# Moving the first batch's result stores from GpSimd's queue to SyncE's in a Fourier mixing and SwiGLU kernel

## The chip, the cores and the metric

The kernel runs on one core of one Trainium2 chip. The core has five engines that run side by side, each with its own in-order stream of instructions: TensorE (matmuls; "PE" in the profile), VectorE (DVE), ScalarE (ACT), GpSimd (POOL) and SyncE (SP, which only issues transfers). "SPq", "ACTq" and "POOLq" are what these engines' sequencers do: waits, and the issue of transfers. The metric is the device time of one execution in microseconds (us); lower is better. All data is float32.

## The reference

The first half filters every channel of every batch along the sequence in the frequency domain; the second half is a SwiGLU block over all tokens.

```python
x: (8, 3008, 256)   filt_r, filt_i: (1505, 256)
X = rfft(x, axis=1)
Y = X * (filt_r + 1j * filt_i)
y = irfft(Y, n=3008, axis=1)             # (8, 3008, 256)

t = y.reshape(24064, 256)
g = t @ w_gate                            # (256, 1536)
v = t @ w_val                             # (256, 1536)
out = (g * sigmoid(g) * v) @ w_out        # (24064, 256), float32
```

## The kernel before, in words

**Work and order.** The eight batches are taken one after the other (index `b`). A batch's sequence of 3008 is handled as 47 x 64, and the SwiGLU half is done on four chunks of tokens (`k` = 0..3) in three groups of hidden features (`g` = 0..2): twelve steps per batch. In batch 0 the order of the first nine steps is by group: chunks 0, 1, 2 of group 0, then of group 1, then of group 2 (steps 6, 7 and 8); chunk 3 follows in steps 9, 10 and 11. In all other batches a chunk's three groups follow each other.

**The written-out schedule.** Within a step the order is a list of tokens, `SCHEDULE`, walked in the last loop. A capital letter is usually a group of matmuls (`P`, `Q`, `A`, `B`, `E` hidden products, L1034; `W` output products, L1131), a small letter the work on another engine that goes with it. A prime means the work of an earlier step. The lines that matter below:

- `D` (L329, on GpSimd) subtracts two tiles that ScalarE made; VectorE's `s` and `x` (L1056) need `D`, and the hidden products `A` (tile `wa`) need those.
- `S` (L326 and L329, on GpSimd) combines hidden tiles `h` for the output products.
- `o` (L326, VectorE) adds output products to the result tile `o`, and `z` (L1102, VectorE) transposes it in 32 x 32 blocks.
- `t` tokens run a piece of the spectral work of the *next* batch. In batch 0, steps 6 to 10, these are `stage2a` (matmuls into `pb`, L870; then VectorE L879, L883, L886 and a GpSimd addition, all on parts of the tile `lent`) and `stage2b` (matmuls into `pc`, L903; ScalarE's copy L911; ScalarE's transfer `d<-lent`, L917). `stage2a` of unit u first calls `load_two` for unit u+1: through `load` (L596) SyncE issues one piece of a table (`later_tbl`), four of `filt_r`, two of `filt_i` and one of the intermediate `d`, all into `lent`. The matmuls of `stage2b` for unit u-2 stand just before those of `stage2a` for unit u. Each of the two uses the same single PSUM bank in turn.
- `i0` to `i11` are the stores of batch 0's finished results. Each is issued two steps after its group, at steps 8, 9, 10 and 13 (step 13 is the second step of batch 1): twelve stores of 30 or 32 rows x 16 x 32 values (60 or 64 KB), each made of runs of 32 values (128 bytes). In batches 1 to 7 the stores belong to other tokens (`x`) and go to SyncE's queue.
- In batch 1's first three steps ScalarE also negates parts of the filter (`negated_filter`): SyncE loads them (L318), ScalarE multiplies them by -1 (L321), SyncE stores them (L323).

**Queues and semaphores.** SyncE issues nearly all loads: weights (`wt_t<-w_all`, L477), saved sums (`y_t<-yt`, L1266), saved outputs (`o<-o`, L996), and those of `load_two`. An engine issues its transfers in the order in which the program records them, and one that waits holds back all behind it. The recording layer gives the transfers of SyncE and ScalarE *together* eight completion semaphores in turn (they are named DMAHW0 to DMAHW7 in the listing of the built program); a transfer that is given a semaphore first waits until the transfer that had it before has landed, which is usually the one eight places earlier in the common order. GpSimd's transfers have eight of their own (DMASW0 to DMASW7).

The choice of the queue, before:

```python
queue = nc.sync if b else nc.gpsimd
if last:
    queue = (nc.sync, nc.scalar, nc.gpsimd)[(2 * p + n) % 3]
```

Of the kernel before, what the change touches and what calls it, by code (L numbers as in the profile page):

```python
# [203 lines left out]
def kernel(  # L204
# [10 lines left out]
    nc = tc.nc  # L215
# [109 lines left out]
    def add(eng, dst, a, b):  # L325
        return eng.tensor_tensor(out=dst, in0=a, in1=b, op=ALU.add)  # L326
# [663 lines left out]
    def takes_turns(b, k):  # L990
        return b == 0 and k < NT

    def new_outs(b, k, g):
        outs[b, k] = opool.tile([128, 4 * NH, RP], FP32, name=f"o_{b}_{k}_{g}", tag="o", bufs=2)
        if g:
            pin(nc.sync.dma_start(out=outs[b, k], in_=o_dram[k]))  # L996
        else:
            pin(nc.gpsimd.memset(outs[b, k][:, :, NR:], 0.0))

    class Group:  # L1000
# [94 lines left out]
        def project(self, op, last=False):  # L1095

            b, k, q = self.b, self.k, self.g
            kind, p = op[0], int(op[1:].split(".")[0])
            if kind == "z":
                if q == NG - 1:  # L1100
                    t = self.part(p)
                    pin(nc.vector.transpose(out=t, in_=t))  # L1102
                return
            if kind in "xXi":
                t, first, count = outs[b, k], 2 * NH * (kind == "X"), 2 * NH if last else 4 * NH
                if kind == "x" and q < NG - 1 and takes_turns(b, k) and p == 5:
                    pin(nc.sync.dma_start(out=o_dram[k], in_=t))
                if q == NG - 1 and (b or kind == "i"):
                    some = (p,) if kind == "i" else (2 * p, 2 * p + 1)
                    for n, (u, cq) in enumerate(divmod(m, 4) for m in some):  # L1110
                        rows = min(32, NR - 32 * u)
                        at = (b * S + 32 * 32 * u + 2 * NH * k) * C + 128 * first + 32 * cq
                        queue = nc.sync if b else nc.gpsimd
                        if last:
                            queue = (nc.sync, nc.scalar, nc.gpsimd)[(2 * p + n) % 3]
                        pin(queue.dma_start(  # L1116
                            out=bass.AP(tensor=out.tensor, offset=out.offset + at,
                                        ap=[[32 * C, rows], [128, count], [1, 32]]),
                            in_=t[32 * cq:32 * cq + rows, first:first + count, ts(u, 32)]))
                return  # L1120
            if kind == "q":
                at, kind, p = "A", "o", 4
            else:
                at = {1: "A", 6: "A", 7: "A", 4: "F" if last else "A", 2: "F", 5: "G",
                      3: "G"}[p]
            if kind == "W":
                start = p in (1, 2, 5) or last and p == 4
                if start:
                    self.bank(at, 3)
                for i in range(JB):  # L1130
                    pin(nc.tensor.matmul(  # L1131
                        out=self.tiles[at], lhsT=wo_t[:, JB * q + i, WO[p], :],
                        rhs=self.hs[i][:, HID[p]], start=start and i == 0,
                        stop=True, skip_group_check=True))
                return
            if q == 0 and p == 1:
                new_outs(b, k, q)
            i, cb = {1: (0, 0), 2: (0, 0), 6: (0, 1), 3: (0, 1), 4: (1, 0), 7: (1, 1),
                     5: (1, 1)}[p]
            dst = self.part(2 * i + cb)[:, :, 0:NR].rearrange("p n (t r) -> p t n r", t=2)  # L1140
            src = self.tiles[at].rearrange("p (t n r) -> p t n r", t=2, n=NH)
            if q == 0 and at == "A":
                pin(nc.scalar.copy(out=dst, in_=src))
            else:
                pin(add(nc.vector, dst, dst, src))
# [316 lines left out]
```

## Time and profile before

The time is 2839.53 us, the median of three runs (2835.15 to 2841.27); the profiled execution has a span of 2837.5 us.

| engine | busy us | share of the span |
|---|---|---|
| PE (matmul) | 2789.6 | 98% |
| PEld (weight load, beside PE) | 2315.4 | 82% |
| DVE | 2035.0 | 72% |
| ACT | 1567.1 | 55% |
| POOL | 1525.2 | 54% |

The stretch in which batch 0's stores are issued is small: GpSimd issues them in four bursts, from 323.9, 359.7, 394.7 and 483.3 us. Steps 8, 9, 10 and 13 begin on TensorE at about 322, 357, 393 and 482 us. A step takes about 29 us where TensorE has no gaps (454.54 to 483.75 on the chain of waits, from one `wqa` to the next).

How to read the views: a timeline row is start, duration, engine, line, operation, output <- input and count, with the idle time just before it and what ended that idle time in brackets. A row of the waits is who waited for whom: total us, times, longest. A row of the chain of waits is start, duration and what ran. A row of the windows is the stretch, its length, then each engine's busy us and number of instructions, the granted TensorE clock (1.00 is full speed), the busy share of the transfer engines and GB/s.

### The profile page before, as it was taken

How to read it: one execution, taken by the hardware profiler on the slowest of the kernel's cores; microseconds unless marked ns; L12 is line 12 of the kernel's file. 1: busy time of each engine (PE TensorE's matmuls, PEld its weight loads, DVE VectorE, ACT ScalarE, POOL GpSimd, SP SyncE). 2: the span in 40 equal slices, each digit the busy share in tenths (PEclk: the TensorE clock that was granted, in tenths of full speed). 3: DMA queues.
4: the chain of work that ended last, by engine and by line, in shares of the span. 5: the costliest groups of instructions: out<-in, count | busy, mean ns of one | idle time of the engine just before them, and what ended most of it. 6: DMA issues, size and time to landing. Idle time of an engine off the chain costs nothing.

```text
span 2837.5 us, 48561 instructions
## 1 busy us (share of the span) xinstructions
PE 2789.6 (98%) x15432; PEld 2315.4 (82%) x15432; DVE 2035.0 (72%) x4603; ACT 1567.1 (55%) x4202; POOL 1525.2 (54%) x1671
## 2 busy tenths in 40 slices
PE   8999999999999999999999999999999999999998
PEld 6777878788888888888888888878888888888887
DVE  6898766767667776677766677667776767766666
ACT  6775445555555555555555555555555555555554
POOL 4886566454545554455544555444554454545543
PEclk9999999999999999999999999999999999999999
DMA  8687867877666775667666676667765777645443
GB/s 231 218 272 251 269 203 228 275 226 233 188 183 204 248 218 178 199 213 232 216 185 197 214 238 204 185 191 234 228 205 177 214 221 226 195 146 153 151 137 82
DMA packets 363372, 586.58 MB, mean 207 GB/s; under 512 B 198388, under 2 KB 246260, under 8 KB 363024
## 3 DMA queue, kind: packets, MB, share of 16 engines
q1 hardware_dynamic: 337922, 534.73, 60.6%
q10 hardware_dynamic: 23406, 45.43, 5.9%
q0 software_dynamic: 1792, 3.34, 0.5%
q8 instruction: 125, 2.05, 0.3%
q14 instruction: 127, 1.04, 0.1%
HBM read 467.87 MB, written 101.34 MB: 201 GB/s over the span
## 4 chain that ended last, share of the span: by engine, by line
PE 85%; DVE 4%; POOL 3%; issue 2%; DMA 1%; ACT 1%; SPq 0%; ACTq 0%; DVEq 0%; POOLq 0%
PE wa L1034 22%; PE wk L1034 16%; PE wA L1131 15%; PE we L1034 12%; PE wG L1131 8%; PE wF L1131 4%; PE pd L937 3%; PE wqa L690 2%; PE wqc L749 1%; PE wqb L761 1%; POOL out_dram L1116 1%; DVE y L333 1%; DVE lent L818 1%; POOL h L329 1%; DVE o L326 0%
## 5 line engine op out<-in xcount | busy, mean ns | idle before, releaser
L1034 PE MATMUL wa<-y_t,wt_t 128*128 128x188 f32 x4464 | 880.3, 323 | 6.3 <-DVE wa L1056 2.0
L1034 PEld LDWEIGHTS wa<-y_t,wt_t 128*128 128x128 f32 x4464 | 746.8, 190 | 84.9 <-ACT wa L1060 11.0
L1034 PEld LDWEIGHTS wk<-y,wt_t 128*128 128x128 f32 x2976 | 494.6, 190 | 106.7 <-issue 33.4
L1034 PE MATMUL wk<-y,wt_t 128*128 128x188 f32 x2976 | 571.3, 325 | 0.3 <-ACT f L1049 0.3
L329 POOL TENSOR_TENSOR h<-h 128x376 f32<-128x376 f32 x572 | 558.0, 998 | 15.4 <-DVE h L326 15.2
L326 POOL TENSOR_TENSOR h<-h 128x376 f32<-128x376 f32 x190 | 183.6, 988 | 707.0 <-DVE h L1081 696.7
L1131 PE MATMUL wA<-h,wo_t 128*128 128x376 f32 x1532 | 552.6, 483 | 4.0 <-DVE o L326 3.8
L1034 PE MATMUL we<-y_t,wt_t 128*128 128x188 f32 x2232 | 434.0, 324 | 7.0 <-DVE we L333 4.1
L329 POOL TENSOR_TENSOR D<-f,f 128x376 f32<-128x376 f32 x288 | 280.0, 987 | 254.5 <-ACT f L1049 254.4
L329 DVE TENSOR_TENSOR we<-we,m 128x376 f32<-128x376 f32 x576 | 318.7, 554 | 121.3 <-PE we L1034 63.7
L1034 PEld LDWEIGHTS we<-y_t,wt_t 128*128 128x128 f32 x2232 | 368.4, 190 | 12.8 <-DVE we L333 8.2
L1131 PEld LDWEIGHTS wA<-h,wo_t 128*128 128x128 f32 x1532 | 275.2, 190 | 115.0 <-issue 12.0
L1069 ACT COPY m<-wa 128x376 f32<-128x376 f32 x576 | 272.9, 474 | 85.4 <-PE wa L1034 82.5
L333 DVE SCALAR_TENSOR_TENSOR y<-wk,c 128x376 f32<-128x376 f32 x480 | 246.5, 540 | 58.7 <-ACT c L1053 36.0
L1076 ACT ACTIVATE g<-wa 128x188 f32<-128x188 f32 x576 | 188.0, 326 | 164.9 <-PE wa L1034 154.6
L1131 PE MATMUL wG<-h,wo_t 128*128 128x376 f32 x768 | 274.0, 479 | 0.0
L1076 ACT ACTIVATE u<-we 128x188 f32<-128x188 f32 x576 | 188.3, 328 | 153.9 <-DVE we L329 147.7
L1053 ACT COPY c<-wk 128x376 f32<-128x376 f32 x288 | 136.4, 474 | 224.6 <-PE wk L1034 196.1
L1049 ACT ACTIVATE f<-wk 128x376 f32<-128x376 f32 x288 | 140.5, 488 | 173.4 <-PE wk L1034 141.7
L1065 ACT COPY we<-y 128x376 f32<-128x376 f32 x480 | 221.8, 480 | 18.1 <-DVE h L1081 13.4
L1081 DVE TENSOR_TENSOR h<-wa,g 128x188 f32<-128x188 f32 x576 | 198.7, 345 | 33.2 <-ACT g L1076 32.9
L1081 DVE TENSOR_TENSOR h<-we,u 128x188 f32<-128x188 f32 x576 | 197.4, 344 | 29.8 <-ACT u L1076 19.0
(162 smaller groups left out, 3518.0 us busy)
## 6 DMA issues: line engine op xcount, KB each, us to landing
wt_t<-w_all SPq DMA_DIRECT2D x174, 896.0 KB, 4.6
wt_t<-w_all SPq DMA_DIRECT2D x174, 768.0 KB, 4.5
lent<-filter SPq DMA_DIRECT2D x36, 1024.0 KB, 7.0
lent<-d SPq DMA_DIRECT2D x84, 256.0 KB, 4.3
d<-lent ACTq DMA_DIRECT2D x84, 256.0 KB, 3.9
d<-lent ACTq DMA_DIRECT2D x96, 192.0 KB, 3.1
lent<-raw SPq DMA_DIRECT2D x144, 128.0 KB, 2.1
t<-d SPq DMA_DIRECT2D x112, 128.0 KB, 4.6
```

What stands on the lines that cost most here:

```text
L326: return eng.tensor_tensor(out=dst, in0=a, in1=b, op=ALU.add)
L329: return eng.tensor_tensor(out=dst, in0=a, in1=b, op=ALU.subtract)
L333: return nc.vector.scalar_tensor_tensor(out=dst, in0=a, scalar=-1.0, in1=b, op0=ALU.mult, op1=ALU.subtract)
L937: pin(nc.tensor.matmul(out=rows, lhsT=self.t4[k, i][:, j, ts(cb, 128)], rhs=cols, start=j == 0, stop=True, skip_group_check=True))
L1034: pin(nc.tensor.matmul(out=ps[:, z], lhsT=self.wt[:, SLOT[p], z], rhs=rhs, start=start and z == 0, stop=True, skip_group_check=True))
L1049: pin(act.mul(self.small(f"f{i}", f"f{i}", 1), t[f"k{i}"], -1.0))
L1053: pin(act.copy(out=self.small(f"c{i}", f"c{i}", 1), in_=t[f"k{i}"]))
L1065: pin(act.copy(out=self.bank(f"e{at}"), in_=t[f"y{at}"]))
L1069: pin(act.copy(out=self.small(f"m{at}", "m", 4), in_=t[f"a{at}"]))
L1076: pin(act.activation(out=self.small(op, "g", 3, 1)[:, 0], in_=ps[:, 1], func=AF.Silu))
L1081: pin(v.tensor_tensor(out=dst, in0=ps[:, 0], in1=g, op=ALU.mult))
L1131: pin(nc.tensor.matmul(out=self.tiles[at], lhsT=wo_t[:, JB * q + i, WO[p], :], rhs=self.hs[i][:, HID[p]], start=start and i == 0, stop=Tru ...
```

## The change

Batch 0's stores are issued from SyncE's queue, as those of the other batches are. It is for GpSimd, which computes on `h`, `D` and `lent` in the same steps: it then has no transfers to issue there. What is stored, from where, to where and at which token stays the same. The last projection's stores (`last`) keep their three queues.

```diff
                         at = (b * S + 32 * 32 * u + 2 * NH * k) * C + 128 * first + 32 * cq
-                        queue = nc.sync if b else nc.gpsimd
+                        queue = nc.sync if b else nc.sync
                         if last:
                             queue = (nc.sync, nc.scalar, nc.gpsimd)[(2 * p + n) % 3]
```

## The prediction
> **What bounds the kernel now.** I read the page first, then GpSimd's stores, the chain of waits, and the engines' timelines from 322 to 425 us and from 480 to 515 us.
>
> ```profile
> PE 2789.6 (98%) x15432; PEld 2315.4 (82%) x15432; DVE 2035.0 (72%) x4603; ACT 1567.1 (55%) x4202; POOL 1525.2 (54%) x1671
> ...
> PE 85%; DVE 4%; POOL 3%; issue 2%; DMA 1%; ACT 1%; SPq 0%; ACTq 0%; DVEq 0%; POOLq 0%
> ```
>
> TensorE is the bound: only a gap or a slow stretch of TensorE that comes or goes moves the time. The change touches steps 8, 9, 10 and 13, some 130 us of 2838.
>
> The chain of waits, steps 8 and 9:
>
> ```profile
> 327.92 1.95 POOL h L329 x2
> 329.87 2.53 POOL out_dram L1116 x4
> 332.40 1.00 POOL D L329
> ...
> 362.36 1.95 POOL h L329 x2
> 364.31 2.53 POOL out_dram L1116 x4
> 366.84 1.00 POOL D L329
> ```
>
> The stores stand between GpSimd's `h` and `D`, and `D` leads to VectorE's L1056 and TensorE's `wa`. TensorE's timeline there:
>
> ```profile
> 334.89 1.51 PE L1034 MATMUL wa<-y_t,wt_t 128*128 128x188 f32 x8 [1.59 <-DMA y_t<-yt]
> ...
> 340.38 1.03 PE L903 MATMUL pc<-lent 128*128 128x256 f32 x4
> ...
> 346.33 1.03 PE L870 MATMUL pb<-lent 128*128 128x256 f32 x4
> ...
> 368.48 1.54 PE L1034 MATMUL wa<-y_t,wt_t 128*128 128x188 f32 x8 [1.03 <-DVE wa L1056]
> ...
> 381.33 2.04 PE L903 MATMUL pc<-lent 128*128 128x256 f32 x4 [2.22 <-DVE lent L886]
> ```
>
> Gaps of one to two microseconds follow the bursts. The windows show a slower clock after two of them:
>
> ```profile
> 338.00:342.00 4.00, 4.00 (x16) 3.30 (x15) 3.15 (x8) 1.36 (x3) 3.98 (x6) 0.72 1.00 355
> 380.00:384.00 4.00, 2.67 (x7) 2.33 (x8) 3.52 (x8) 1.66 (x5) 1.27 (x1) 0.65 0.28 117
> ```
>
> The last three numbers are clock, busy share of the transfer engines, GB/s. SyncE's queue is tight too:
>
> ```profile
> 368.33 4.40 SPq L596 DMA_DIRECT2D lent<-in_filt_i_dram  x2
> 372.78 0.43 SPq L596 DMA_DIRECT2D lent<-d  x1
> ```
>
> and its waits from 364 to 376 us:
>
> ```profile
> SPq L596 <- DMA d<-lent: 3.0, 1, 3.0
> ```
>
> These two loads have free buffers. The second takes the semaphore that ScalarE's `d<-lent` of 366.21 holds, and stands until that lands, about 372.4. So SyncE can be held up by a ScalarE transfer that has nothing to do with its load.
>
> **What the Trainium skill says.** "DMA: Bandwidth & Descriptors", section "Issuing engines are not separate DMA queues": all queues share the same 16 transfer engines, and another issuing engine saves only sequencer time. In the trace a store takes GpSimd 0.652 us (median) to issue and SyncE 0.490 us. The same page, section "Anatomy of one DMA": "any semaphore wait happens on the issuing sequencer before dispatch"; the 4.40 us above agree. "TensorE: Matmul & The Clock Gate", section "What's actually happening": an idle window of about 3.4 us halves the clock. Here 1.59 us plus 0.32 us, and 2.22 us, went with a mean clock of 0.72 and 0.65 over the 4 us around; a gap costs more than its length.
>
> **The change part by part.**
>
> *Removed from GpSimd:* 12 stores x 0.652 = 7.8 us in each of four steps. In step 13 none stood on the chain, so that burst brings nothing. In step 8 the gap at 334.89 was ended by a reload of `y_t` issued at 329.38, which stays; I give TensorE at most 2 us there (1.1 of this gap, as fewer stores share the transfer engines ahead of the reload, and some of the slow clock). In step 9 the gaps 1.03 + 0.40 + 0.21 + 2.22 = 3.9 us go, and about 1.3 us of slow clock (380 to 388 us: 0.65 and 0.92). In step 10, 0.16 + 0.59 + 0.40 = 1.15 us go. Together at most 8.3 us.
>
> *Added to SyncE:* 12 x 0.490 = 5.9 us of issue per step, and, what counts more, 12 more users of the eight semaphores shared with ScalarE. The order of the program's waits can be read from the listing of the built changed kernel (number on SyncE, line, transfer, semaphore waited for):
>
> ```
> 262 L477 DMACopy wt_t<-w_all 128x1792 [waits DMAHW0, PE]
> 263 L596 DMACopy lent<-later_tbl 128x512 [waits DMAHW1]
> 270 L596 DMACopy lent<-d1_1 128x2x256 [waits DMAHW0]
> 310 L596 DMACopy lent<-in_filt_r_dram 32x512 [waits DMAHW3]
> ```
>
> Following each semaphore back to its previous user gives what matters:
>
> 1. Step 8. The reload `wt_t` (262) now waits for ScalarE's `d<-lent` that follows `pc` of 340.38. Before, its semaphore's last user was an old filter load, and it was issued at 331.70. Behind it stands the whole load of a unit (`later_tbl`, filters, `d`), and this unit's `d` (270) waits in turn for `wt_t` to land. The matmul `pb` of 346.33 needs that `d`. Before, `d` was issued at 342.34, just in time. Working it out: `pc` comes at about 338.4; ScalarE issues `d<-lent` 1.7 us later as before (342.06 - 340.38): 340.1; landing 3.3 us (before, one issued at 326.11 released SyncE at 329.38): 343.4; `wt_t` lands 4.6 us on (median of page part 6): 348.0; `d` in a further 3 to 4.3 us (4.3 its median; the queues are empty by then): 351 to 352.3. I take 351: `pb` is 4.7 us later than before. Bounds: 349 (+2.8) with the shortest landings, 354 (+7.7) with the longest.
> 2. Step 9. The unit's second `filt_r` (310) now waits for ScalarE's `d<-lent` behind `pc` of 381.33. Before, this unit was loaded at 365.59 to 372.78, well before its `pb` of 388.96. Now: `pc` at 379.1 without its gap, plus 4.7 from step 8, less 1.6 of earlier gaps: 382.2; `d<-lent` issued 383.9, landed 387.2; five more issues of about 0.45 us: `d` at 389.4, landed 393.4. The `pb` is 4.4 us late against before, where without this wait it would stand near 0: step 9 gives back what it gained.
> 3. Step 10. SyncE's stores stand between weight reloads that wait for TensorE anyway (16.60 us for three of them from 401.44), so they cost nothing; the gain of 1.1 us holds: +3.3.
> 4. Step 13. The stores stand between the loads of L318. The chain before:
>
> ```profile
> 501.22 5.63 DMA lent<-in_filt_i_dram
> ...
> 509.01 0.90 PE we L1034 x4
> ```
>
> ScalarE waits at L321 for this load with almost no slack (TensorE's gap at 509.01 is 0.20 us), and behind L321 stand ScalarE's copies that TensorE needs. Of the twelve stores, five stand where SyncE waited anyway (482.8 to 489.5, for ScalarE's `d<-lent`); of the rest four or five fall ahead of this load, 2 us of issue, and the second four loads now wait until the first four have landed (four apart with the stores between, instead of old loads of `x`). I take +3 us; bounds 1 and 5.
> 5. The clock. Two new gaps of 5 to 6 us should dip it at least as the gaps of 2 us did (1.3 to 1.7 us each), in place of dips that I have counted as gone or that lie in what the chain covers; +1.2 net.
>
> On the transfer engines themselves little changes: same bytes, and with 57% to 70% of their time in SyncE's queue they were not full over these stretches. At the kernel's end, where all three queues store 32 KB pieces, eight of SyncE's took 9.9% of 16 us and eight of GpSimd's 7.5%: 0.20 against 0.15 us each, so 12 x 0.1 = 1.2 us per step for 64 KB; in steps 8 and 13 it is inside the landings taken above.
>
> Sum: 4.7 at step 8, 4.4 after step 9, 3.3 after step 10, 6.3 after step 13, 7.5 with the clock. 2839.5 + 7.5 = 2847.0 us. Nothing later absorbs it: TensorE runs without a gap through most of the later steps.
>
> **The rivals.**
>
> *The same (chance 0.30, about 2840).* The waits exist, but `d<-lent` and `wt_t` land faster in emptied queues, and the losses of steps 8 and 13 (+2.8, +1) only eat the gains (-2 to -3 that survive in steps 9 and 10). For it: SyncE's landings scatter from 2 to 8 us. Against: three landings in a row must all be short.
>
> *Faster (0.08, about 2833).* GpSimd was the only limit, SyncE has room, and most of the 8.3 us come: 2839.5 - 6.5. For it: the chain names GpSimd's stores. Against: before, `d` came just in time at 346.33, and the listing puts new waits ahead of it.
>
> *Much slower (0.12, about 2858).* The gaps halve the clock for longer, or ScalarE's `d<-lent` is itself held by the late loads, and each of steps 8, 9 and 13 loses 6 us. Against: in the listing ScalarE's transfers wait only for loads that come long before.
>
> **How the numbers follow.** The forecast, somewhat slower, has 0.50; its time is 2847.0. It lies above the bound of 2845.2 (0.2%) in most of its spread. Chances: faster 0.08; same 0.31; slower 0.61. The range reaches from 2836 (gains hold, small losses) to 2857 (step 8 at +7.7, step 9 nothing gained, step 13 at +5, two dips of 1.7), leaving out most of the faster rival and the end of the slowest.
>
> **What would show it.** In the changed kernel: no GpSimd stores from 323 to 498 us, `D` of step 9 about 4 us sooner after its `h`; SyncE idle in step 8 before `wt_t` for several us with `d<-lent` as releaser; TensorE gaps of 4 to 7 us before a `pb` (L870) in step 8 and of 3 to 5 us in step 9, with a load into `lent` as releaser, and clock dips after; a gap of 2 to 5 us in step 13 before `we`, released by ScalarE. I am wrong if `pb` of step 8 comes at 346 or before, or if `wt_t` is issued before ScalarE's `d<-lent`.

## The result, and the profile after

The changed kernel takes 2849.7 us (median of four runs, 2849.28 to 2851.59) against 2840.4 us before: a ratio of 1.0037, with an interval of 1.0022 to 1.0052. It is slower by some 10 us (6 to 15). The page of the changed kernel, its busy times, its two queues and its chain:

```profile
PE 2790.9 (98%) x15432; PEld 2318.8 (81%) x15432; DVE 2035.0 (71%) x4603; ACT 1565.1 (55%) x4202; POOL 1493.9 (52%) x1623
...
q1 hardware_dynamic: 362738, 537.81, 61.3%
...
q0 software_dynamic: 256, 0.25, 0.0%
...
PE 83%; DVE 2%; issue 1%; DMA 1%; SPq 0%; ACT 0%; POOL 0%; POOLq 0%; DVEq 0%; ACTq 0%
```

GpSimd has lost 31 us of work and is gone from the chain (3% before), as intended. TensorE's busy time has grown by 1.3 us of the span's 10.2, so most of what was lost is gaps. TensorE's timeline shows the largest three in the steps that the change touches (last column: idle time before, and its releaser):

```profile
352.90 2.05 PE L870 MATMUL pb<-lent 128*128 128x256 f32 x4 [8.74 <-DMA out_dram<-o]
...
394.86 1.10 PE L870 MATMUL pb<-lent 128*128 128x256 f32 x4 [2.77 <-issue]
...
515.99 1.62 PE L1034 MATMUL we<-y_t,wt_t 128*128 128x188 f32 x4 [3.12 <-ACT we L1065]
```

They lie in steps 8, 9 and 13. The windows after the first and the third (the last three numbers are clock, busy share of the transfer engines, GB/s):

```profile
350.00:354.00 4.00, 1.10 (x3) 0.95 (x4) 0.00 (x0) 0.00 (x0) 0.00 (x0) 0.50 0.93 204
354.00:358.00 4.00, 4.00 (x14) 3.82 (x13) 2.25 (x5) 0.51 (x2) 0.00 (x0) 0.50 0.92 290
...
516.00:520.00 4.00, 4.00 (x12) 3.47 (x13) 2.04 (x6) 1.16 (x5) 0.31 (x1) 0.59 0.99 356
```

The clock is at half until 358.8 us, 5.9 us of it after the gap of 8.74 us has ended. What this costs is read from the distance of two neighbouring groups, `pb` to the next `pc`: 9.24 us (352.90 to 362.14), where it was 6.24 before, so 3.0 us on top of the gap. The Trainium skill ("TensorE: Matmul & The Clock Gate", "What's actually happening") has an idle window of about 3.4 us halve the clock; this gap is over twice that, and the trace agrees (0.50). But a gap of 2.65 us in e2_steps9_10, shorter than that window, was followed by half clock too (0.50, last section); there the measurement decides.

The chain of waits of the changed kernel in step 8:

```profile
338.22 0.88 PE pc L903 x4
...
339.12 0.59 ACT lent L911
...
339.73 5.43 DMA d<-lent
...
345.23 0.34 SPq L477
...
345.62 5.05 DMA lent<-later_tbl
...
350.69 2.21 DMA out_dram<-o
...
352.90 2.05 PE pb L870 x4
```

This is the prediction's step 1 piece by piece: `pc`, ScalarE's `d<-lent`, then SyncE's `wt_t` (L477), then the unit's loads, then `pb`. The views name a store as the last releaser, but `pb` doesn't read what a store writes. It needs `d`, which SyncE issued at 349.81 and which landed 3.0 us later, just then. A chain names one path. Whether another was nearly as long it doesn't tell, and here one was (e6_d_pool below).

### The profile page after: what moved, and what is told of

It reads as the page before. It is cut to its first block, busy times and chain, and to the rows that moved or that the text cites. A ratio compares the mean times of both kernels' runs of the same rounds, so it can differ in the third digit from the quotient of the medians.

```text
span 2847.7 us, 48535 instructions
## 1 busy us (share of the span) xinstructions
PE 2790.9 (98%) x15432; PEld 2318.8 (81%) x15432; DVE 2035.0 (71%) x4603; ACT 1565.1 (55%) x4202; POOL 1493.9 (52%) x1623
## 3 DMA queue, kind: packets, MB, share of 16 engines
q1 hardware_dynamic: 362738, 537.81, 61.3%
## 4 chain that ended last, share of the span: by engine, by line
PE 83%; DVE 2%; issue 1%; DMA 1%; SPq 0%; ACT 0%; POOL 0%; POOLq 0%; DVEq 0%; ACTq 0%
PE wa L1034 22%; PE wk L1034 16%; PE wA L1131 15%; PE we L1034 11%; PE wG L1131 8%; PE wF L1131 4%; PE pd L937 3%; PE wqa L690 2%; PE wqc L749 1%; PE wqb L761 1%; DVE lent L818 1%; DMA lent<-in_filt_i_dram 0%; DVE y L333 0%; DVE o L326 0%; DVE h L1081 0%
## 5 line engine op out<-in xcount | busy, mean ns | idle before, releaser
L1034 PE MATMUL we<-y_t,wt_t 128*128 128x188 f32 x2232 | 435.2, 324 | 11.5 <-ACT we L1065 7.4
L1131 PEld LDWEIGHTS wA<-h,wo_t 128*128 128x128 f32 x1532 | 275.0, 190 | 113.1 <-issue 11.1
```

What stands on the lines that cost most here:

```text
L1034: pin(nc.tensor.matmul(out=ps[:, z], lhsT=self.wt[:, SLOT[p], z], rhs=rhs, start=start and z == 0, stop=True, skip_group_check=True))
L1131: pin(nc.tensor.matmul(out=self.tiles[at], lhsT=wo_t[:, JB * q + i, WO[p], :], rhs=self.hs[i][:, HID[p]], start=start and i == 0, stop=Tru ...
```

## The experiments

Three theories stood at the start. A, the prediction's: the stores put loads behind transfers that share their semaphores, ScalarE's `d<-lent` above all, and the clock adds to the gap. B: the time that SyncE takes to issue the stores is the cost. C: it is the packets or bytes of the stores on the transfer engines.

Every kernel was timed beside the kernel before on the same chip, in five rounds. Besides the time I use the length of four stretches in each profile, from a matmul group to the same group in the next kernel: step 8 from `pc` (324.35 before) to `pb` (358.58), step 9 from there to `pb` (388.96), step 10 from there to `wqa` (454.46), step 13 from `wqa` (483.68) to `wqa` (513.65). Here is all of it in one table, us; "before" and "change" are the two kernels of the case.

| kernel | stores of step 8, 9, 10, 13 on SyncE | `d<-lent` | time | ratio, interval | step 8 | 9 | 10 | 13 |
|---|---|---|---|---|---|---|---|---|
| before | none | ACT | 2839.6 to 2840.4 | 1 | 34.23 | 30.38 | 65.50 | 29.97 |
| change | all | ACT | 2849.7 | 1.0037, 1.0022 to 1.0052 | 43.14 | 26.71 | 63.96 | 34.19 |
| e1_step8 | 8 | ACT | 2847.5 | 1.0028, 1.0017 to 1.0040 | 42.22 | 28.88 | 65.49 | 30.11 |
| e2_steps9_10 | 9, 10 | ACT | 2838.1 | 0.9994, 0.9986 to 1.0003 | 33.91 | 26.59 | 65.64 | 29.93 |
| e3_step13 | 13 | ACT | 2844.4 | 1.0016, 1.0009 to 1.0023 | 34.78 | 30.39 | 65.48 | 34.29 |
| e4_tiny | none, 12 tiny ones added in 8 | ACT | 2844.3 | 1.0018, 1.0011 to 1.0025 | 39.13 | 28.72 | 65.48 | 29.95 |
| e5_small | all, 1/16 of the bytes | ACT | 2837.9 | 0.9997, 0.9989 to 1.0005 | 38.00 | 23.78 | 63.86 | 31.79 |
| e6_d_pool | all | POOL | 2842.6 | 1.0008, 1.0000 to 1.0015 | 41.01 | 23.78 | 63.88 | 35.28 |
| e7_d_pool_k012 | 8, 9, 10 | POOL | 2837.8 | 0.9993, 0.9985 to 1.0001 | 39.94 | 23.78 | 63.88 | 29.99 |
| e8_step10 | 10 | ACT | 2839.4 | 0.9994, 0.9987 to 1.0000 | 33.79 | 28.72 | 63.88 | 30.01 |
| e9_d_small | all, 1/16 of the bytes | POOL | 2836.4 | 0.9985, 0.9977 to 0.9994 | 35.24 | 23.77 | 63.87 | 31.34 |
| e10_d_k12 | 9, 10 | POOL | 2832.0 | 0.9968, 0.9957 to 0.9980 | 32.54 | 23.77 | 63.89 | 30.89 |
| e11_d_none | none | POOL | 2843.6 | 1.0010, 1.0003 to 1.0016 | 32.93 | 31.10 | 68.08 | 30.64 |

A stretch is read from one profile each. Where a kernel leaves step 9 alone it was still between 28.72 and 30.39, so about 1.7 us there is scatter; step 10's stretch repeats within 0.03 us in six kernels. Step 8's scatters by up to 1.1 us between kernels that do the same there (change and e1_step8, e6_d_pool and e7_d_pool_k012).

### One step at a time

```diff
-queue = nc.sync if b else nc.gpsimd
+queue = nc.sync if b or k == 0 else nc.gpsimd        # e1
+queue = nc.sync if b or k in (1, 2) else nc.gpsimd   # e2
+queue = nc.sync if b or k == 3 else nc.gpsimd        # e3
+queue = nc.sync if b or k == 2 else nc.gpsimd        # e8
```

Step 8 alone. 

> Only chunk 0's twelve stores (step 8) go to SyncE's queue; the other 36 stay with GpSimd. Theory A (semaphores shared by SyncE and ScalarE: the reload wt_t of step 8 waits for ScalarE's d<-lent, and the unit behind it comes late): the gap before pb of step 8 is there, 7 to 9 us, with a slow clock after it; step 9, where GpSimd's stores are back, takes back some 2 to 4 us because GpSimd has caught up meanwhile; time +4 to +8 us against before. Theory B (SyncE's issue time, 12 x 0.49 us, delays the loads behind it): gap of 3 us at most, time +1 to +3. Theory C (more packets of 128 bytes load the transfer engines): gap of 1 to 2 us, time +0 to +2.

Steps 9 and 10. 

> Only chunks 1 and 2's stores (steps 9 and 10) go to SyncE's queue. Theory A: GpSimd's gaps of step 9 and 10 vanish (3.9 and 1.1 us, and the slow clock of 1.3 us), but a filter load of step 9 now waits for ScalarE's d<-lent behind pc, and pb of 388.96 stays within 2 us of where it was; time -3 to +2 us. Theory B or C: the gains come nearly whole, since SyncE waits for TensorE's reloads there anyway; time -4 to -6 us.

Step 13 alone. 

> Only chunk 3's stores (step 13, in batch 1) go to SyncE's queue. Theory A: TensorE's gap before we grows from 0.2 to about 3 us in step 13 and from 1.7 to about 3.3 us in step 14, each with slow clock after it, because the loads of L318 stand behind stores that wait for ScalarE's d<-lent; time +5 to +8 us. Theory B: 12 x 0.49 us of issue at most, of which half is hidden: +1 to +3 us in step 13 and nothing in step 14. Theory C: +0 to +1.

Step 10 alone. 

> Only step 10's twelve stores from SyncE. Theory A: 1.1 us of TensorE gaps behind GpSimd go, no load waits for ScalarE in that step: 2838.0 to 2839.6. Theory B: 5.9 us of issue ahead of the next loads, 2841 to 2845. Theory C: no loads are delayed where SyncE waits for buffers anyway, 2838 to 2840.

By their medians against 2839.64 us, step 8 alone costs 7.9 us, step 13 alone 4.7, and steps 9 and 10 give back 1.5. The sum, 11.1, lies within the interval of the change (6 to 15), and the stretches of steps 8, 9 and 13 are within 1 us of the change's: nothing speaks for a tie between the steps, and the loss is made in 8 and 13. Step 13's 4.7 lies between the two theories' ranges (5 to 8 and 1 to 3). In step 10 alone the stretch gets 1.6 us shorter, though the time of the whole can't tell that from none. In steps 9 and 10 together the gain is smaller than GpSimd's gaps; TensorE's timeline of e2_steps9_10 shows why:

```profile
387.40 1.40 PE L870 MATMUL pb<-lent 128*128 128x256 f32 x4 [2.65 <-issue]
```

It is the gap that the changed kernel has before its `pb` of 394.86. The next `pc` follows 8.02 us later (395.42), where it was 6.26: another 1.8 us to the clock, and the reason why step 10's stretch, which begins at this `pb`, is no shorter here. Step 13 alone, TensorE's timeline of e3_step13:

```profile
517.12 1.41 PE L1034 MATMUL we<-y_t,wt_t 128*128 128x188 f32 x4 [3.13 <-ACT we L1065]
```

It is the same gap as in the change. The chain of the changed kernel says what is behind it:

```profile
507.93 6.15 DMA lent<-in_filt_i_dram
...
514.15 0.04 ACT lent L321
...
515.99 1.62 PE we L1034 x4
```

This load of L318 was issued 17.5 us after `wqa` before (501.22 less 483.68) and landed in 5.63 us; here it is 19.9 us (507.93 less 488.03) and 6.15 us, together 2.9 us later, which is the growth of the gap before `we` (0.20 to 3.12).

### Twelve tiny stores more in step 8

GpSimd keeps all real stores; SyncE gets, beside each of step 8's, one store of 128 bytes a row into a scratch tensor.

```diff
+if b == 0 and k == 0:
+    pin(nc.sync.dma_start(out=scratch[...], in_=t[32 * cq:32 * cq + rows, 0:1, ts(u, 32)]))
```

> All stores stay with GpSimd as before; beside each of the twelve of step 8, SyncE also stores one run of 128 bytes from each row (32 or 30 rows) of the same tile into a scratch tensor. SyncE so has the same twelve more transfers to issue and twelve more users of the shared semaphores, but a sixteenth of the bytes, and in this program's order the reload wt_t of step 8 waits for one of the small stores and not for ScalarE's d<-lent. Theory A: the large gap does not come; pb of step 8 at most 2 us later than before, time within -1 to +2.5 us. Theory B: as the full change does at step 8, pb later by 5 us or more.

The answer fell between the two. In TensorE's timeline of e4_tiny

```profile
349.23 2.04 PE L875 MATMUL pb<-lent 128*128 128x256 f32 x4 [3.60 <-DMA lent<-d]
```

the gap is 3.60 us, and `pc` follows 9.11 us later, in place of 6.24: the clock lost 2.9 us here too, as much as after a gap of 8.7. So being queued behind a dozen more transfers, with hardly a byte in them, costs 4.9 us of the 8.9 of step 8, over half of that through the clock. `wt_t` stood behind no ScalarE transfer in this kernel, so theory A as I had it, the wait for ScalarE alone, was not the whole.

### The bytes, and ScalarE's transfer

Two more things were varied: how much each store carries, and who issues `d<-lent`. In e5_small each store of batch 0 writes one 128-byte piece of each row.

```diff
+count = 1 if b == 0 else count
```

> All of the changed kernel's stores, issued from the same queue at the same lines, but each of the first batch's stores writes only the first 128-byte piece of each of its 32 rows: fifteen sixteenths of the first batch's results are left out, and with them about 480 of the 512 packets of each store. Theory A (shared semaphores, the order of loads behind ScalarE's d<-lent, and the slow clock behind the gap): the waits are the same in number, so most of the loss stays: a gap of 4 to 9 us before pb in step 8, time 2844 to 2850. Theory B (only SyncE's time of issue): same as the change, 2848 to 2851. Theory C (the many 128-byte packets fill the transfer engines and delay the landings): the loss goes with the bytes, gap before pb under 2 us, time 2837 to 2841.

In e6_d_pool GpSimd issues the second batch's `d<-lent` of units 5 and up, so that SyncE's loads in steps 8 to 10 find none of ScalarE's transfers on their semaphores.

```diff
 queue = nc.scalar if self.b or u >= 8 else nc.sync
+if self.b == 1 and u >= 5:
+    queue = nc.gpsimd
```

> The changed kernel, with the second batch's d<-lent transfers of units 5 and up issued from GpSimd's queue in place of ScalarE's, so that in steps 8 to 10 SyncE's loads have no ScalarE transfer to wait for. Theory A: the gap before pb in step 8 falls from 8.7 to 0 to 3.5 us (what the twelve more users of the semaphores alone cost in the run with tiny stores), the clock stays above 0.6, step 9 needs no wait for d<-lent; steps 13 and 14 lose as before, some 4 to 7 us: time 2841 to 2846. Theories B and C (issue or bytes): SyncE issues the same and the same bytes are moved, so nothing is won: 2848 to 2851.

Both edits together are e9_d_small. 

> The run with d<-lent on GpSimd and all stores on SyncE, and of each of the first batch's stores only the first 128-byte piece of each row: fifteen sixteenths of the first batch's results are left out. SyncE's order and waits in step 8 are those of that run; only the bytes behind each store differ. Theory A+B (in step 8 only the place in the queue, the issue and the semaphores cost): wt_t is still issued at about 340 and lands 9 us later, gap before pb 6 to 8 us, time 2840 to 2843. Theory C (what is left of step 8's loss is the stores' packets ahead of wt_t and of this unit's loads on the transfer engines): wt_t is issued 2 to 3 us sooner and lands in 4.5 to 6 us, gap before pb 0 to 3 us, time 2833 to 2837.

e5_small gave a mixed answer: its time, 2837.9 us, is the one that theory C expected, but its gap before `pb` of step 8 is theory A's:

```profile
348.08 2.04 PE L870 MATMUL pb<-lent 128*128 128x256 f32 x4 [5.17 <-DMA out_dram<-o]
```

In e6_d_pool the wait for ScalarE's transfer is gone and the time is in theory A's range, but the gap of step 8 stayed, against its expectation. In TensorE's and SyncE's timelines of e6_d_pool (its lines stand 2 lower from L913 on)

```profile
351.91 2.04 PE L870 MATMUL pb<-lent 128*128 128x256 f32 x4 [7.79 <-DMA out_dram<-o]
```

```profile
338.10 1.63 SPq L1118 DMA_DIRECT2D out_dram<-o  x3
339.83 0.53 SPq L477 DMA_DIRECT2D wt_t<-w_all  x1
...
344.73 0.84 SPq L596 DMA_DIRECT2D lent<-in_filt_i_dram  x2
348.80 0.39 SPq L596 DMA_DIRECT2D lent<-d  x1
```

`wt_t` follows the stores at once, and so does the rest of the load, but the last piece, `d`, stands until 348.80, as it shares `wt_t`'s semaphore. That is 9.0 us after the issue of `wt_t`; in the changed kernel, where `wt_t` came late into nearly empty queues (0 to 23 GB/s from 343.7 to 345.9 us), `d` could go 4.6 us after it:

```profile
329.98 5.02 SPq L1116 DMA_DIRECT2D out_dram<-o  x6
...
338.08 1.59 SPq L1116 DMA_DIRECT2D out_dram<-o  x3
345.23 0.34 SPq L477 DMA_DIRECT2D wt_t<-w_all  x1
...
349.81 0.39 SPq L596 DMA_DIRECT2D lent<-d  x1
```

So a second cause lay beside ScalarE's transfer, and it alone makes most of the gap. The bytes tell what it is. e9_d_small has e6_d_pool's order in this step, only with 1/16 of the bytes in the stores; its TensorE and SyncE:

```profile
350.26 2.04 PE L870 MATMUL pb<-lent 128*128 128x256 f32 x4 [2.92 <-DMA out_dram<-o]
```

```profile
333.49 2.93 SPq L1119 DMA_DIRECT2D out_dram<-o  x6
...
340.19 0.34 SPq L477 DMA_DIRECT2D wt_t<-w_all  x1
...
346.80 0.39 SPq L596 DMA_DIRECT2D lent<-d  x1
```

This profile is 4 us later in step 8 than the other (`pc` at 328.75, there 324.76), so `wt_t` is issued 3.6 us sooner after `pc`, and `d` 2.4 us sooner after that. Most of the first part lies in SyncE's own issue instructions: the first six stores take it 2.93 us here, 5.02 in the change and 5.38 in e6_d_pool. So theory B's issue time and theory C's bytes are not two separate things: the issue of full stores lasts longer. Why, no view says. The transfer engines over the 11.5 us that begin with the first store (queue: packets, MB, share of 16 engines), e6_d_pool and then e9_d_small:

```profile
q1 hardware_dynamic: 3939, 2.03, 75.0%
```

```profile
q1 hardware_dynamic: 1521, 3.08, 79.6%
```

Two thirds of the bytes in two and a half times the packets keep the engines as busy. The Trainium skill ("DMA: Bandwidth & Descriptors", "Specifications") wants pieces of at least 512 bytes for the full rate; these stores are made of 128-byte pieces, and the two lines agree. Whether the number of packets or their bytes matters more I did not separate.

From `pc` of 324.35 to `pb` of 346.33, 21.98 us before, the corners are as follows. Where several kernels do the same in step 8, all are given, since their spread is the scatter.

| step 8, `pc` to `pb` | full stores on SyncE | 1/16 of the bytes | no store on SyncE |
|---|---|---|---|
| `d<-lent` on ScalarE | 27.89 (change), 27.14 (e1) | 24.19 (e5_small) | 21.98 (before), 21.58 (e2), 22.45 (e3), 21.46 (e8) |
| `d<-lent` on GpSimd | 27.15 (e6_d_pool), 25.67 (e7) | 21.51 (e9_d_small) | 20.25 (e10), 20.59 (e11) |

The bytes are worth 3.0 to 5.6 us. ScalarE's transfer is worth 2.7 us with small stores (in e5_small it is not `wt_t` but a filter load of the same unit that waits for it) and 0 to 2.2 with full ones, where kernels that do the same differ by up to 1.5, so with full stores its share is not clear of the scatter. Without either, `pb` comes no later after `pc` than before, and about 1 us later than with no store on SyncE, which is within the scatter. TensorE, which gets there sooner than before, still waits 2.92 us for it.

Step 13 answers to the bytes too, but in lesser part: its stretch is 34.19 to 35.28 with full stores on SyncE, 31.34 and 31.79 with small ones, 29.93 to 30.89 with none. Its gap before `we`, 0.20 us before and 3.12 in the change, is still 2.31 in e5_small and 1.86 in e9_d_small:

```profile
505.89 0.91 PE L1034 MATMUL we<-y_t,wt_t 128*128 128x188 f32 x4 [2.31 <-ACT we L1065]
```

```profile
507.55 0.90 PE L1036 MATMUL we<-y_t,wt_t 128*128 128x188 f32 x4 [1.86 <-ACT we L1067]
```

The load of L318 is issued 19.5 us after `wqa` in both, against 17.5 before and 19.9 in the change. So most of this gap comes from the stores' places in SyncE's queue and the waits that go with them. After these shorter gaps the clock stayed at 1.00, and in the change TensorE ran at half clock from 515.99 to 519.3, which is another 1.6 us of the difference.

In step 9 a filter load waits for ScalarE's transfer, as predicted. SyncE's waits of the changed kernel from 380 to 394 us:

```profile
SPq L596 <- DMA d<-lent: 5.9, 1, 5.9
```

In e6_d_pool, all stores still on SyncE, the filter loads go through in 2.60 us in place of 7.56, TensorE has no gap in step 9, and the stretch is 23.78, 2.9 us shorter. (It is as short in e5_small, where ScalarE's transfers stay: with small stores the filter loads take 3.27 us, so that wait ends early enough, and the bytes have a share in this loss too.)

### A version that beats both

Stores in step 8 and 13 cost, in 9 and 10 they gain once ScalarE's transfer is out of the way. e7_d_pool_k012 leaves step 13 to GpSimd, e10_d_k12 steps 8 and 13; e11_d_none is the kernel before with `d<-lent` moved to GpSimd and no store moved.

```diff
+queue = nc.gpsimd if b == 0 and k == 3 else nc.sync   # e7
+queue = nc.sync if b or k in (1, 2) else nc.gpsimd    # e10
+queue = nc.sync if b else nc.gpsimd                   # e11
```

> As the run with d<-lent on GpSimd, and the twelve stores of step 13 stay on GpSimd: SyncE takes those of steps 8, 9 and 10 only. Theory A: what is won in steps 9 and 10 (some 4 to 5 us) stands against 0 to 5 us in step 8, and steps 13 and 14 lose nothing: 2836 to 2842. Theories B and C: three steps of the change's loss, 2845 to 2849.

> Stores of steps 9 and 10 on SyncE, those of steps 8 and 13 on GpSimd, and the second batch's d<-lent of units 5 and up on GpSimd. If each step's loss and gain stand by themselves: step 8 and 13 as before, step 9 some 4 to 6.6 us shorter, step 10 some 1.6 us: 2832 to 2836. If d<-lent among GpSimd's work delays its h or D again: 2837 to 2840.

> The kernel before with only the second batch's d<-lent of units 5 and up moved from ScalarE's queue to GpSimd's; all the first batch's stores stay on GpSimd. If the gain of the runs with d<-lent on GpSimd comes from the stores' move: 2838.5 to 2841, the gaps of steps 9 and 10 as before. If d<-lent on ScalarE was itself a loss in the kernel before: 2834 to 2838.

e10_d_k12 takes 2832.0 us, 8.3 less than before (0.9957 to 0.9980 of it). Neither half does that: the stores of steps 9 and 10 alone gave 0.9994, and `d<-lent` on GpSimd alone was slower, 1.0010. For e11_d_none both expectations missed; TensorE's timeline shows that a GpSimd that also has the stores delays `D`, and with it VectorE's L1058 (L1056 before):

```profile
369.44 2.87 PE L1036 MATMUL wa<-y_t,wt_t 128*128 128x188 f32 x8 [2.57 <-DVE wa L1058]
...
406.48 2.87 PE L1036 MATMUL wa<-y_t,wt_t 128*128 128x188 f32 x8 [2.36 <-DVE wa L1058]
```

The first gap was 1.03 us before and the second 0.59. With the stores off GpSimd in these two steps both are gone, and so is the load's wait: each move makes room for the other.

## Why the prediction held, point by point

The forecast of 2847.0 us and "slower" stands 2.7 us below the measured 2849.7, within its range. That it is so close is partly luck: the loss of step 8 was sized some 3 us too small (4.7 and a share of the clock's 1.2, measured 8.9), and step 9's gain about as much too small (0.3, measured 3.7). Two of the predicted signs were missed in size: the gap before `pb` of step 8 was 8.74 us where 4 to 7 were named, that of step 9 2.77 us where 3 to 5 were. The parts came out so:

- **GpSimd freed.** Stepwise right. In step 9 `D` goes straight after `h`; the run from the second `h` to the last `D`s takes 5.6 us (369.31 to 374.86) in place of 9.4 (362.36 to 371.78). The gaps before `wa` and `pc` in steps 9 and 10 are gone. The gain was sized at 5.2 us in step 9; with all waits taken out the stretch is 6.6 us shorter than before, of which 1.7 may be scatter.
- **Step 8, the size.** `pb` was to come 4.7 us later; it came 5.9 later (21.98 to 27.89). `wt_t` did wait for ScalarE's `d<-lent`, but that took 5.43 us to land where I took 3.3; `d` landed 3.0 us after its issue, the short end of what I took.
- **Step 8, the reason.** This is the step that failed. The prediction held ScalarE's transfer to be what delays `wt_t`, and put the stores' packets on the transfer engines at 1.2 us per step, "inside the landings". e6_d_pool takes the transfer away and `pb` gains 0.7 us, which is not clear of the scatter; e9_d_small takes the bytes away too and gains 5.6 more. The place behind nine stores and their packets delays the load nearly as much as the transfer did; the two run side by side, and the sum came out because only the longer counts.
- **The clock.** Right as a net, wrong in its places. Predicted was +1.2 us net, from dips of 1.3 to 1.7 us after two new gaps, in steps 8 and 9. By the count of the last section TensorE lost 3.0 us to half clock after the gap of step 8, nothing in step 9, and 1.6 in step 13, where no dip was named. Before, it had lost 1.7 in step 8 and 1.6 in step 9. The net over these steps is +1.3. As other gaps made it than those named, and step 9's old dip had been counted as gone once already, in the gain of 5.2 us, the agreement is luck.
- **Step 9.** The wait of the second `filt_r` was right in place and releaser, and mis-sized: it costs 2.9 us. The step's net was predicted at -0.3 (4.7 to 4.4) and is -3.7 (-2.0 against the shortest step 9 that GpSimd's stores left elsewhere, 28.72).
- **Step 10.** Predicted -1.1, measured -1.5 in the change and -1.6 alone.
- **Step 13.** Predicted +3, measured +4.2 in the change, +4.3 alone, through the load and the ScalarE copies that were named. Of this the gap before `we` is 2.9 us, so the size was right; the rest fits the half clock after it. The reason given was issue time and semaphores. The small stores, with the same issues, keep 1.7 to 2.1 us of the gap, so it holds for most of it; the rest of the gap, and with it the half clock, came only with the full bytes.

Sum of the profiles: 8.9 - 3.7 - 1.5 + 4.2 = 7.9 us. The two profiled spans differ by 10.2; another 3.35 stand in step 14, which the prediction did not name (29.53 to 32.88 between two `wqa`), and about 1 us comes back elsewhere. In step 14 the gap before `we` grew from 1.66 to 3.32 us, and half clock followed (0.50 from 550 to 553 us). The loss in step 14 is not shown to be the change's: with step 13's stores on GpSimd the same stretch was 29.53 to 33.32 in eight kernels, with them on SyncE 29.63 to 33.98 in five.

The rival "faster" is refuted by e1_step8 and e3_step13: SyncE had room for issuing, but no room ahead of loads that come just in time. "The same" failed as the three landings were not all short: the last was (3.0 us), the first was longer than taken (5.43). "Much slower" had each of steps 8, 9 and 13 lose 6 us; step 8 lost more than that, step 13 less, and step 9 gained.

## What to carry to other kernels

Before moving transfers to a queue with idle time, ask which load behind them comes just in time, what shares their semaphores, and how many small packets they put ahead of that load: a queue may have issue time to spare and still no room in its order. When the chain names one wait, take that wait out before believing that it is the cost, since a second path may end hardly sooner. And decide step by step: here the same move lost in two steps and gained in two, and the gain came in full only when another transfer took the place that was left free.

## What the runs showed of the hardware

- Moving the 48 stores took 1536 packets out of GpSimd's queue (1792 to 256) and put 24816 more into SyncE's (337922 to 362738), for the same 3.1 MB: 32 records per store in one queue, 517 in the other, for the same store.
- The issue of the same store on SyncE did not take a fixed time. In the first six stores of step 8 one instruction took 0.48 to 2.09 us in the change and 0.42 to 0.61 in e9_d_small, with 1/16 of the bytes.
- The clock's price did not follow the length of the gap. It is half of the time for which TensorE works while the clock is at half. The windows of 1 us show how long that is; here are those of e2_steps9_10 (clock third from the end), which add up to 3.4 us at half:

```profile
388.00:389.00 1.00, 1.00 (x5) 0.83 (x4) 0.16 (x1) 0.00 (x0) 0.00 (x0) 0.54 0.99 416
389.00:390.00 1.00, 1.00 (x5) 1.00 (x4) 0.97 (x2) 0.00 (x0) 0.00 (x0) 0.50 1.02 419
390.00:391.00 1.00, 1.00 (x5) 1.00 (x4) 0.61 (x2) 0.33 (x1) 0.00 (x0) 0.50 0.96 401
391.00:392.00 1.00, 1.00 (x6) 1.00 (x6) 0.65 (x2) 0.00 (x0) 0.00 (x0) 0.76 1.02 386
```

The same count for five gaps; "lost" is what the way from `pb` to the next `pc` takes over the 6.24 to 6.26 us of an undisturbed pair:

| kernel, step | gap, us | half clock | TensorE working in it, us | half of that | lost |
|---|---|---|---|---|---|
| change, 9 | 2.77 | none | 0 | 0 | 0.1 |
| e2_steps9_10, 9 | 2.65 | 388.1 to 391.5 | 3.4 | 1.7 | 1.8 |
| e4_tiny, 8 | 3.60 | 348.1 to 354.9 | 5.7 | 2.8 | 2.9 |
| e6_d_pool, 8 | 7.79 | 348.2 to 355.0 | 3.1 | 1.6 | 1.6 |
| change, 8 | 8.74 | 348.6 to 358.8 | 5.9 | 3.0 | 3.0 |

Half clock came here for 3.4, 6.8 or 10.2 us, and what of it fell into the gap itself cost nothing: 3.7 us in e6_d_pool, 4.3 in the change. When it sets in after a gap, and for how long, no run here tested.
